# A four-stage transformer kernel whose fourth GEMM is computed by seven half-size products for eight

## The chip, the cores and the metric

The kernel runs on one core of a Trainium2 chip. The metric is the device time of one execution in microseconds, lower is better; each of the runs below is one measurement of it, and the profile is one execution recorded by the hardware profiler.

## The reference

Float32 attention with 32 global tokens and a local window feeds a gated block, and that feeds a second one. Batch 4, 8 heads of 64, 512 local and 32 global tokens: 2176 tokens of 512 features after attention.

```python
attn = concat([softmax(q_g @ k_all.T / 8) @ v_all,
               softmax([q_l @ k_g.T / 8, mask(q_l @ k_l.T / 8)]) @ [v_g, v_l]])
x = attn as rows of 512
h = x @ w_in                       # first GEMM, 512 -> 1024
s = h * softmax(h)
y = layernorm(s) * g_ln @ w_out    # second GEMM, 1024 -> 512
h = y @ w2_in                      # third GEMM, 512 -> 2048
g = h * clip(h + 3, 0, 6) / 6
out = g @ w2_out                   # fourth GEMM, 2048 -> 512
```

## The kernel before

The 2176 tokens are 17 units of 128 (16 local, one global). A unit passes through attention, the first GEMM (L804), the softmax product and the layer norm, and the second GEMM (L864, whose left operand comes by DMA transposes `lT<-l`, issued on SP). The weights lie in DRAM as 64-bit words; `decode` (L404 to L422) makes float32 of a loaded block of 512 columns with one ScalarE and several VectorE or GpSimd instructions, `norm` (L436) sums its squares, `power_scale` (L366 to L375, with the tiny matmul of L372 that adds over partitions) makes a power of two of the sum, and `split` (L444 to L456) makes two float16 values, a high part and a rest, of each number. With such pairs a product is three terms: high x high, high x rest, rest x high.

The third and fourth GEMMs are in `second(gi)` (L950 to L1006). The units are taken in `GROUPS` of 4, 4, 3, 3, 3. For each group, 16 chunks `f` of 128 of the 2048 features are gone through: 12 matmuls of the third GEMM (L968; 4 slices of 128 features x 3 terms, 512 or 384 token columns) fill a PSUM tile `S`; ScalarE makes relu(h + 3) of it (L972), VectorE min(., 6) x h (L974), ScalarE the high half (L977), VectorE the rest (L979); the fourth GEMM (L988) adds 3 terms per unit, of 512 output columns each, into one accumulator bank per unit (tags V, V, Y, Y). After the last chunk the accumulators are scaled (L1003 on VectorE, L1005 on ScalarE) and stored (L1006). Group 0 does its fourth GEMM with fp32r pairs; `convert` (L938 to L948) makes float16 pairs of those weights for groups 1 to 4, in buffers of earlier stages, after `token_scale` has one scale of all tokens. `prep_w2(f)` (L881 to L908) prepares chunk `f` of both weights.

The order on every engine is set by class `Plan`: each step has an engine, a cost, what it reads and writes, the buffers it needs and a rank, and a list scheduler places steps by rank as their inputs, buffers and engines come free. A table `RK` of ranks, `MODE` strings (which engine or variant a block gets) and `SLOTS` (how many buffers) are constants of the file. All loads, transposes and stores are issued on SP's one queue, in the planned order.

## Time and profile before

| | us |
|---|---|
| three runs | 724.06, 727.26, 728.14 |
| median | 727.26 |
| span of the profiled execution | 722.6 |
| TensorE (PE) busy in it | 668.1 |
| VectorE (DVE) busy | 456.6 |
| ScalarE (ACT) busy | 410.3 |
| GpSimd (POOL) busy | 166.7 |

The profiled execution's own time is not given beside its span. Busy time counts matmuls, copies and the like, not waits or the issue of DMAs. A line name such as L968 is a line of the kernel before; `S<-ybig,w2i` reads output, then inputs. A matmul's row gives the time from its start to its modelled end, and since matmuls overlap, the price of one in a stream is the distance to the next. The mean granted clock of TensorE over the span is 0.974 of full speed.

### The profile page before, as it was taken

How to read it: one execution, taken by the hardware profiler on the slowest of the kernel's cores; microseconds unless marked ns; L12 is line 12 of the kernel's file. 1: busy time of each engine (PE TensorE's matmuls, PEld its weight loads, DVE VectorE, ACT ScalarE, POOL GpSimd, SP SyncE). 2: the span in 40 equal slices, each digit the busy share in tenths (PEclk: the TensorE clock that was granted, in tenths of full speed). 3: DMA queues.
4: the chain of work that ended last, by engine and by line, in shares of the span. 5: the costliest groups of instructions: out<-in, count | busy, mean ns of one | idle time of the engine just before them, and what ended most of it. 6: DMA issues, size and time to landing. Idle time of an engine off the chain costs nothing.

```text
span 722.6 us, 11985 instructions
## 1 busy us (share of the span) xinstructions
PE 668.1 (92%) x4488; PEld 412.6 (57%) x4488; DVE 456.6 (63%) x1112; ACT 410.3 (57%) x783; POOL 166.7 (23%) x197
## 2 busy tenths in 40 slices
PE   3665789999999999989999999999999999999997
PEld 2443465676766777566666666444455555555553
DVE  4799878886767788796879987933323233323323
ACT  6767658766566787667667776423333333324323
POOL 7243236531613153633421420000000000000000
PEclk9998759999999999999999999999999999999999
DMA  9998976999799979872835410100010000001001
GB/s 317 251 255 175 213 157 181 212 187 207 202 224 189 173 154 176 140 187 81 197 77 175 146 59 17 43 1 0 1 59 0 1 20 26 0 1 44 1 1 44
DMA packets 155657, 82.93 MB, mean 115 GB/s; under 512 B 132944, under 2 KB 141136, under 8 KB 155600
## 3 DMA queue, kind: packets, MB, share of 16 engines
q1 hardware_dynamic: 155600, 82.18, 48.6%
q8 instruction: 35, 0.57, 0.3%
q14 instruction: 22, 0.18, 0.1%
HBM read 42.55 MB, written 4.46 MB: 65 GB/s over the span
## 4 chain that ended last, share of the span: by engine, by line
PE 75%; DMA 9%; DVE 6%; ACT 4%; issue 2%; POOL 1%; SPq 1%; ACTq 0%; DVEq 0%; POOLq 0%
PE S L968 22%; PE V L988 14%; PE Y L988 10%; PE Y L864 10%; PE H L804 8%; PE S L609 5%; DMA PT<-zone 4%; PE S L644 2%; DMA lT<-l 2%; PE V L736 1%; DMA wd<-in_vm_dram 1%; DVE tm L812 1%; DMA raw<-in_w_in_dram 1%; DMA zone<-in_ki_dram 1%; DVE zone L634 1%
## 5 line engine op out<-in xcount | busy, mean ns | idle before, releaser
L968 PE MATMUL S<-ybig,w2i 128*128 128x384 f16 (+1 forms) x720 | 139.4, 347 | 0.0
L972 ACT ACTIVATE g<-S,three,inv 128x384 f32<-128x384 f32 (+1 forms) x80 | 56.9, 712 | 135.3 <-PE S L968 133.9
L974 DVE SCALAR_TENSOR_TENSOR g<-g,S 128x384 f32<-128x384 f32 (+1 forms) x80 | 48.2, 605 | 126.0 <-ACT g L972 123.8
L968 PEld LDWEIGHTS <-w2i 128*128 128x128 f16 x720 | 69.8, 98 | 63.0 <-issue 2.2
L988 PEld LDWEIGHTS <-gh 128*128 128x128 f16 x624 | 60.6, 98 | 71.7 <-ACT gh L977 3.6
L864 PE MATMUL Y<-lT,wout 128*128 128x256 f16 (+1 forms) x864 | 96.0, 269 | 2.8 <-DMA lT<-l 2.8
L804 PE MATMUL H<-win,xT 128*128 128x512 f16 x384 | 91.8, 386 | 2.2 <-DVE tm L817 1.2
L864 PEld LDWEIGHTS <-wout 128*128 128x128 f16 x864 | 80.3, 99 | 16.2 <-issue 2.8
L979 DVE SCALAR_TENSOR_TENSOR gh<-g,g_scale,gh 128x384 f16<-128x384 f32 (+1 forms) x64 | 41.7, 651 | 41.9 <-ACT gh L977 27.5
L609 PE MATMUL S<-zone 64*128 64x224 f32 x256 | 58.9, 439 | 8.4 <-ACT sg L650 7.0
L977 ACT ACTIVATE gh<-g,g_scale 128x384 f16<-128x384 f32 (+1 forms) x64 | 41.0, 641 | 41.0 <-DVE g L974 41.0
L804 PEld LDWEIGHTS <-xT 128*128 128x128 f16 x384 | 36.2, 99 | 45.5 <-issue 9.0
L619 ACT ACTIVATE e<-e,sa 128x224 f32<-128x224 f32 x128 | 53.1, 471 | 14.3 <-DVE sa L614 14.1
L609 PEld LDWEIGHTS S<-zone 64*128 64x128 f32 x256 | 38.9, 222 | 21.5 <-ACT sg L650 8.5
L614 DVE CUSTOM_DVE_ANT_0 e<-msk,S 128x224 f32<-128x224 f32 x128 | 42.9, 381 | 12.8 <-PE S L609 12.0
L968 PE MATMUL S<-ybig,zone 128*128 128x384 f16 (+1 forms) x240 | 47.2, 347 | 0.0
L988 PE MATMUL V<-raw,gh 128*128 128x512 f16 x144 | 42.8, 379 | 0.0
L634 DVE SCALAR_TENSOR_TENSOR zone<-e,zone 128x896 f16<-128x896 f32 x32 | 36.2, 1130 | 5.4 <-ACT zone L632 2.8
L686 PE MATMUL V<-v,PT 128*128 128x65 f16 x128 | 25.6, 203 | 14.6 <-DMA PT<-zone 14.6
L988 PE MATMUL V<-wd,gh 128*128 128x512 f16 x120 | 35.7, 379 | 0.0
L968 PEld LDWEIGHTS <-zone 128*128 128x128 f16 x240 | 23.3, 98 | 20.9 <-issue 0.6
L644 PE MATMUL S<-zone 128*128 128x128 f32 (+1 forms) x128 | 27.2, 344 | 7.8 <-DVE sa L614 7.6
(226 smaller groups left out, 1297.0 us busy)
## 6 DMA issues: line engine op xcount, KB each, us to landing
raw<-in_w_in_dram SPq DMA_DIRECT2D x24, 512.0 KB, 4.4
raw<-in_w_out_dram SPq DMA_DIRECT2D x24, 512.0 KB, 4.2
zone<-in_ki_dram SPq DMA_DIRECT2D x16, 448.0 KB, 4.2
out_dram<-o SPq DMA_DIRECT2D x17, 256.0 KB, 2.1
zone<-in_qi_dram SPq DMA_DIRECT2D x16, 256.0 KB, 3.0
wd<-in_vm_dram SPq DMA_DIRECT2D x12, 256.0 KB, 4.7
vs<-v SPq DMA_DIRECT2D x24, 64.5 KB, 2.6
vs<-vg SPq DMA_DIRECT2D x16, 64.5 KB, 2.9
```

What stands on the lines that cost most here:

```text
L609: T.matmul(out=S()[:, j], lhsT=p.tile(qk)[d, 2 * hf + j], rhs=p.tile(kk)[d, 2 * hf + j], start=True, stop=True)
L614: V.tensor_tensor_reduce(out=p.tile(ek)[:, KC * (2 * j + jj):KC * (2 * j + jj) + KC], in0=msk[:, mtyp], in1=S()[:, j], scale=-0.125, scala ...
L619: A.activation(out=p.tile(ek)[:, c:c + KC], in_=p.tile(ek)[:, c:c + KC], func=AF.Exp, bias=p.tile(sa)[:, h:h + 1], scale=-1.0)
L634: vop(dve(896), lambda ev=ev, pk=pk: V.scalar_tensor_tensor(out=p.tile(pk)[:, 1, :, 0:KC], in0=ev(), scalar=PSC, in1=p.tile(pk)[:, 0, :, 0 ...
L644: T.matmul(out=p.tile(gk)[:, 0:n], lhsT=p.tile(gq)[:, 2 * hf + j], rhs=p.tile(kk)[:, 2 * hf + j, 0:n], start=(j == 0), stop=(j == 1))
L804: T.matmul(out=p.tile(hk)[:, 512 * n:512 * n + 512], lhsT=(p.tile(xk) if xb else xgT)[:, 4 * a + k], rhs=win16[:, w, k, 512 * n:512 * n + ...
L864: T.matmul(out=Y()[:, m2], lhsT=wout16[:, w, k, 128 * m:128 * m + 128], rhs=p.tile(lk)[:, 8 * a + k, 0:n], start=(z == 0 and k == 0), stop ...
L968: T.matmul(out=p.tile(hk)[:, 0:n], lhsT=p.tile(wk)[:, w, k], rhs=y16[:, a, k, c0:c0 + n], start=(z == 0 and k == 0), stop=(z == 2 and k == 3))
L972: aop(act(n, 2), lambda hk=hk, gk=gk, iv=iv: A.activation(out=p.tile(gk)[:, 0:n], in_=p.tile(hk)[:, 0:n], func=AF.Relu, bias=three, scale= ...
L974: vop(dve(n), lambda hk=hk, gk=gk: V.scalar_tensor_tensor(out=p.tile(gk)[:, 0:n], in0=p.tile(gk)[:, 0:n], scalar=6.0, in1=p.tile(hk)[:, 0: ...
L979: vop(dve(n, 1), lambda rk=rk, gk=gk, gs=gs: V.scalar_tensor_tensor(out=p.tile(rk)[:, 1, 0:n], in0=p.tile(gk)[:, 0:n], scalar=gs, in1=p.ti ...
L988: T.matmul(out=p.tile(accs[t]), lhsT=p.tile(rk)[:, a, 128 * t:128 * t + 128], rhs=p.tile(ok)[:, w], start=(f == 0 and z == 0), stop=(f == ...
```

## The change

The fourth GEMM is done in a Strassen scheme on 2 x 2 blocks. The units are taken in pairs (8 pairs and the single unit 16, `NG` = 9 groups), and the chunks in pairs too (8 pairs, `pi`). For one chunk pair and one pair of units, the product of a 2 x 2 arrangement of blocks (two units by two chunks) with another (two chunks by two halves of 256 output columns) is formed from 7 products of a sum of token blocks with a sum of weight blocks, instead of 8 products of single blocks. Each product is 3 matmuls of 256 columns (the three float16 terms). Seven accumulators of 256 columns fill four banks, called a, b (tags V) and d, c (the two halves of the former tile H of the first GEMM, so they exist only after it).

- The sums on the token side are made by VectorE (L1051: 128, 256 and 256 columns), so that high part (L1060) and rest (L1062) have 896 columns in place of 512. The sums on the weight side, five of 256 columns per chunk pair, are made in the preparation (VectorE or GpSimd by a mode string), and a pair's weights are split into nine blocks.
- The work is in two phases of four chunk pairs (`PHASES`). Phase 0 goes through all groups with chunk pairs 0 to 3 and stores scaled partial sums to DRAM (`part`, L1160); phase 1 goes through them again with chunk pairs 4 to 7, loads the partial sums (`pp`, L1110) and adds them. The weights of pairs 4 to 7 are prepared during phase 0, which frees the memory that nine blocks a pair need.
- At the end of a phase of a pair of units, ten instructions combine the seven sums (ScalarE L1137 and L1138 for a and d, VectorE L1139 to L1157, in phase 1 two adds on GpSimd, L1146 and L1149).
- A mode string says which of the 18 group-phases are quick: 15 are; one pair of phase 0 and the single unit (both phases) keep single blocks of 512 columns (L1091).
- There is no fp32r and no conversion any more. The token scale is taken twice, of units 0 to 3 and of units 4 to 16. The scale of each chunk's output weights needs its own tiny matmul (16 more).
- The third GEMM's matmuls have 256 token columns (a pair of units), 24 per chunk pair and group (L1031).
- Planned costs of GpSimd and of a DMA's latency are raised, and all ranks and modes are new, so the order before the second blocks changes too.

```diff
-GROUPS = [(0, 4), (4, 4), (8, 3), (11, 3), (14, 3)]
+PHASES = [(0, 4), (4, 4)]
+TOKENS = [(0, 4), (4, 17)]
+NP = NF // 2
+NG = NU // 2 + 1
...
+    for z in range(2):
+        p.tag(f"H{z}", [p.slots["H"]["tiles"][0][:, 512 * z:512 * z + 512]], "hb")
...
+        for c, (x, y, op) in enumerate([((0, 1), (1, 0), ALU.add), ((0, 1), (0, 0), ALU.add), ((1, 1), (1, 0), ALU.add), ((0, 0), (1, 0), ALU.subtract), ((1, 1), (0, 1), ALU.subtract)]):
+            on, cost, E = (vop, dve(256), V) if MODE["wc"][pi] == "v" else (gop, pool2(256), G)
+            on(cost, lambda E=E, c=c, x=x, y=y, op=op: E.tensor_tensor(out=p.tile(ck)[:, c], in0=half(*x), in1=half(*y), op=op), r=dk, w=[ck], b=[ck] + dk, rank=rank)
...
+    PRODUCTS = {2: ("a", 0, 2, 1), 5: ("a", 1, 3, 7), 1: ("d", 0, 1, 2), 4: ("b", 0, 6, 6), 3: ("b", 1, 0, 5), 6: ("c", 0, 4, 3), 7: ("c", 1, 5, 4)}
+    BANKS = dict(a="V", b="V", c="H0", d="H1")
...
+        units = [2 * q, 2 * q + 1] if 2 * q + 1 < NU else [2 * q]
+        nu = len(units)
...
+            for f in range(2):
+                for z, ch in enumerate(passes(4)):
+                    def mm(f=f, z=z, ch=ch, h=h, wk_=wi[f]):
+                        for k, a, w in ch:
+                            T.matmul(out=h()[:, f], lhsT=p.tile(wk_)[:, w, k], rhs=y16[:, a, k, c0:c0 + n], start=(z == 0 and k == 0), stop=(z == 2 and k == 3))
...
+                for o, x, y, op in (((2, 1, 1), (1, 1, 1), (7, 1, 1), ALU.add), ((3, 2, 1), (0, 2, 1), (7, 2, 1), ALU.add), ((5, 2, 1), (0, 2, 8), (1, 2, 6), ALU.subtract)):
...
+                src = lambda gk=gk: p.tile(gk)[:, 128:1024]
+                m = 896
...
+                def mm4(ms, zs, rk=rk, wk=wk, at=at, last=last):
+                    for m_ in ms:
+                        bk, half, ai, bi = PRODUCTS[m_]
+                        for z in zs:
+                            a, w = TERMS[z]
+                            T.matmul(out=p.tile(bank[bk])[:, 256 * half:256 * half + 256], lhsT=p.tile(rk)[:, a, 128 * ai:128 * ai + 128], rhs=p.tile(wk)[:, w, bi],
+                                     start=(at == 0 and z == 0 and half == 0), stop=(last and z == 2), skip_group_check=True)
...
+                    for ms, bk in (((2, 5), "a"), ((1,), "d"), ((4, 3), "b"), ((6, 7), "c")):
+                        pe(3 * len(ms) * mm16(256), lambda mm4=mm4, ms=ms: mm4(ms, range(3)), r=[rk, wk] + before, w=[("oo", key, bk)], b=[rk, wk] + accs, rank=rank + 0.5)
...
+            if ph:
+                gop(pool2(512), lambda: G.tensor_tensor(out=ob(1, 2), in0=ev(0, 2), in1=pb(1, 2), op=ALU.add), r=sx + [pk], w=[("sp", key)], b=[ek, ok, pk], rank=rank)
...
+        for z, u in enumerate(units):
+            to = out if ph else part
+            dma(262144, lambda z=z, u=u, to=to: SP.dma_start(out=to[u], in_=p.tile(ok)[:, z]), r=[("of", key, z)], w=[("st", ph, q, z)], b=[ok], rank=rank)
...
+        if u == SLOTS["AT"]:
+            prep_w2i(0, RK["w2"], "V")
+            prep_w2o(0, RK["w2"] + 0.1, "V")
...
+    for pi in range(1, 4):
+        prep_w2i(pi, RK["w2z"] + 2 * pi, "V")
+        prep_w2o(pi, RK["w2z"] + 2 * pi + 0.1, "V")
+    for pi in range(4, NP):
+        prep_w2i(pi, RK["w2b"] + 4 * pi, "Y")
+        prep_w2o(pi, RK["w2b"] + 4 * pi + 0.1, "Y")
...
+    for ph in range(2):
+        for q in range(NG):
+            second(ph, q)
```

TensorE in the fourth GEMM (`gh` are the split token sums, `ws` the weights of a chunk pair; a row is one matmul or its weight load). Before, in a middle group of three units:

```order
L988 LDWEIGHTS gh0_3598
L988 MATMUL V0_71<-zone_102,gh0_3598 128x512
L988 LDWEIGHTS gh0_3598
L988 MATMUL V1_72<-zone_102,gh0_3598 128x512
L988 LDWEIGHTS gh0_3598
L988 MATMUL Y1_75<-zone_102,gh0_3598 128x512
```

and after, the first six of the seven products of one term in a middle chunk pair of phase 1, where V1 is bank a, V0 bank b, and H0 the tile of d and c:

```order
L1074 MATMUL V1_72<-ws6_0_4606,gh_0_3740 128x256
L1074 LDWEIGHTS gh_0_3740
L1074 MATMUL V1_72<-ws6_0_4606,gh_0_3740 128x256
L1074 LDWEIGHTS gh_0_3740
L1074 MATMUL H0_73<-ws6_0_4606,gh_0_3740 128x256
L1074 LDWEIGHTS gh_0_3740
L1074 MATMUL V0_71<-ws6_0_4606,gh_0_3740 128x256
L1074 LDWEIGHTS gh_0_3740
L1074 MATMUL V0_71<-ws6_0_4606,gh_0_3740 128x256
L1074 LDWEIGHTS gh_0_3740
L1074 MATMUL H0_73<-ws6_0_4606,gh_0_3740 128x256
```

Three banks of whole units have become products of half the columns; at the last chunk pair of a phase they come product by product: a, d, b, c, with d and c on the same tile.

VectorE at the end of a group. Before, one eviction stands between the chunks of the next group:

```order
L974 SCALAR_TENSOR_TENSOR g2_3595<-g2_3595,S1_70 128x384
L979 SCALAR_TENSOR_TENSOR gh1_3599<-g2_3595,g_scale_150,gh1_3599 128x384
L1003 TENSOR_SCALAR o4_3604<-V1_72,inv6_147 128x512
L974 SCALAR_TENSOR_TENSOR g0_3593<-g0_3593,S0_69 128x384
L979 SCALAR_TENSOR_TENSOR gh0_3598<-g0_3593,g_scale_150,gh0_3598 128x384
```

and after, at the end of a quick group of phase 1 (`ev` holds evicted sums, `inv6` the scale):

```order
L1041 SCALAR_TENSOR_TENSOR g_0_3738<-g_0_3738,S0_69 128x2x256
L1051 TENSOR_TENSOR g_0_3738<-g_0_3738 128x128
L1051 TENSOR_TENSOR g_0_3738<-g_0_3738 128x256 x2
L1139 SCALAR_TENSOR_TENSOR ev_0_3745<-V0_71,inv6_1_1_236,ev_0_3745 128x256
L1141 SCALAR_TENSOR_TENSOR ev_0_3745<-V0_71,inv6_1_1_236,ev_0_3745 128x256
L1155 SCALAR_TENSOR_TENSOR ev_0_3745<-H0_73,inv6_1_1_236,ev_0_3745 128x256 x2
L1147 SCALAR_TENSOR_TENSOR o_1_3744<-V0_71,inv6_1_1_236,o_1_3744 128x512
L1062 SCALAR_TENSOR_TENSOR gh_2_3742<-g_0_3738,acol1_1_235,gh_2_3742 128x896
L1157 TENSOR_TENSOR o_1_3744<-ev_0_3745 128x256 x2
```

The evictions of c (from H0) and b (from V0) stand between the next chunk pair's sums and its rest.

SP's queue behind the last transpose of the second GEMM's operand. Before, the last 15 weight loads follow one another:

```order
L845 DMA_TRANSPOSE lT_97<-l_95 128x16x128
L398 DMA raw_83<-in_w_out_dram 128x1024
L398 DMA raw_84<-in_w_in_dram 128x4x256
L398 DMA raw_85<-in_w_out_dram 128x1024
L398 DMA raw_83<-in_w_in_dram 128x4x256
L398 DMA raw_84<-in_w_out_dram 128x1024
```

and after, they are spread between stores and loads of partial sums:

```order
L849 DMA_TRANSPOSE lT_99<-l_97 128x16x128
L410 DMA raw_83<-in_w_in_dram 128x4x256
L410 DMA raw_84<-in_w_out_dram 128x1024
L410 DMA raw_85<-in_w_out_dram 128x1024
L1160 DMA part<-o_3743 128x512 x2
L1110 DMA pp_4594<-part 128x512
L410 DMA raw_83<-in_w_in_dram 128x4x256
L1110 DMA pp_4594<-part 128x512
L410 DMA raw_84<-in_w_in_dram 128x4x256
L1160 DMA part<-o_3744 128x512 x2
L1110 DMA pp_4595<-part 128x512 x2
```

A weight load now stands behind a store that waits for its group's results.

## Rows read from the trace of the kernel before

**Rows 1.** The page: span, and each engine's busy time, share and instructions.
```profile
span 722.6 us, 11985 instructions
...
PE 668.1 (92%) x4488; PEld 412.6 (57%) x4488; DVE 456.6 (63%) x1112; ACT 410.3 (57%) x783; POOL 166.7 (23%) x197
```

**Rows 2.** Stretches: length; busy us (count) of PE, PEld, DVE, ACT, POOL; clock; DMA share; GB/s.
```profile
0.00:100.00 100.00, 59.06 (x365) 40.54 (x365) 78.28 (x221) 68.11 (x153) 42.07 (x49) 0.89 0.88 228
100.00:370.00 270.00, 260.55 (x2374) 184.69 (x2375) 208.65 (x567) 188.59 (x378) 107.26 (x136) 0.97 0.86 180
370.00:440.00 70.00, 69.93 (x326) 46.23 (x324) 60.72 (x139) 49.56 (x95) 17.36 (x12) 1.00 0.30 98
440.00:460.00 20.00, 20.00 (x93) 10.79 (x91) 19.92 (x45) 17.02 (x27) 0.00 (x0) 1.00 0.15 54
460.00:718.00 258.00, 257.90 (x1337) 130.25 (x1336) 88.27 (x143) 86.28 (x130) 0.00 (x0) 1.00 0.03 11
```

**Rows 3.** Waits of TensorE: total us, times, longest us.
```profile
PE V L686 <- DMA PT<-zone: 14.6, 7, 5.6
PE Y L372 <- DVE am_v L537: 9.0, 1, 9.0
PE S L644 <- DVE sa L614: 7.6, 4, 3.2
```

**Rows 4.** The chain that ended last: start us, us, what.
```profile
448.22 1.40 PE Y L988 x6
...
505.42 5.18 PE S L968 x24
...
570.90 3.90 PE S L968 x24
```

**Rows 5.** TensorE's timeline, 347 to 373 us: start, us, instruction, idle before.
```profile
348.37 10.65 PE L864 MATMUL Y<-lT,wout 128*128 128x256 f16 x96 [0.71 <-DMA lT<-l]
358.86 0.28 PE L372 MATMUL H<-inv,ones 128*128 128x1 f32 x2
...
364.78 5.52 PE L864 MATMUL Y<-lT,wout 128*128 128x128 f16 x96 [1.38 <-DMA lT<-l]
370.14 2.75 PE L968 MATMUL S<-ybig,zone 128*128 128x512 f16 x12
```

**Rows 6.** The last microseconds, all engines.
```profile
717.15 1.46 PE L988 MATMUL V<-junk,gh 128*128 128x512 f16 x6
...
718.65 0.69 ACT L1005 ACTIVATE o<-V,inv 128x512 f32<-128x512 f32 x1 [0.61 <-PE V L988]
```

**Rows 7.** Groups by shape: count, busy us, mean ns, idle before.
```profile
L634 DVE SCALAR_TENSOR_TENSOR zone<-e,zone 128x896 f16<-128x896 f32 x32 | 36.2, 1130 | 5.4 <-ACT zone L632 2.8 <-POOL zone L629 2.3
...
L974 DVE SCALAR_TENSOR_TENSOR g<-g,S 128x512 f32<-128x512 f32 x32 | 21.7, 682 | 37.0 <-ACT g L972 37.0
...
L632 ACT ACTIVATE zone<-e 128x896 f16<-128x896 f32 x19 | 17.9, 943 | 4.7 <-DMA PT<-zone 4.5
...
L871 ACT ACTIVATE ybig<-Y 128x256 f16<-128x256 f32 x2 | 0.8, 383 | 2.5 <-PE Y L864 2.5
```

**Rows 8.** VectorE's timeline, while it decodes weights in group 0.
```profile
402.64 0.42 DVE L411 TENSOR_SCALAR wd<-wd 128x512 int32<-128x512 int32 x1
402.97 0.42 DVE L410 TENSOR_SCALAR wd<-wd 128x512 f32<-128x512 f32 x1
403.31 0.68 DVE L417 SCALAR_TENSOR_TENSOR wd<-raw,wd 128x512 int32<-128x512 int32 x1
403.91 0.42 DVE L411 TENSOR_SCALAR wd<-wd 128x512 int32<-128x512 int32 x1
```

**Rows 9.** All engines, 430.5 to 433 us: VectorE and GpSimd side by side.
```profile
430.57 0.73 DVE L979 SCALAR_TENSOR_TENSOR gr<-g,inv,gr 128x512 fp32r<-128x512 f32 x1
...
431.19 1.29 POOL L354 TENSOR_TENSOR w2o<-wd,w2o 128x512 fp32r<-128x512 f32 x1 [2.94 <-ACT w2o L901]
431.23 1.80 DVE L445 SCALAR_TENSOR_TENSOR w2i<-wd,psc,w2i 128x512 f16<-128x512 f32 x1
```

More of the change, by code (lines that the diff above doesn't have):

```diff
@@ L316, in attention_solu_swish_kernel @@
     zone_at[0] = 0
[L317 removed]
+    carve("ws1", 1, [128, 2, 9, 256], F16, "z")
+    for f in range(2, 8):
         carve(f"w2i{f}", 1, [128, 2, 4, 128], F16, "z")
[L319 removed]
     tags(right1, "e", SLOTS["e"], [128, 4 * KC], F32, "a")
@@ L368, in power_scale, with total @@
             lambda: V.tensor_scalar(out=si[:, 2:3], in0=p.tile(pk).bitcast(I32)[:, 0:1], scalar1=24, scalar2=23, op0=ALU.logical_shift_right, op1=ALU.logical_shift_left),
[L369 to L372 removed]
+            lambda: V.tensor_scalar(out=si[:, 0:1], in0=si[:, 2:3], scalar1=-1.0, scalar2=float((205 - down) << 23), op0=ALU.mult, op1=ALU.add),
+            lambda: V.tensor_scalar(out=si[:, 1:2], in0=si[:, 2:3], scalar1=1.0, scalar2=float((49 + down) << 23), op0=ALU.mult, op1=ALU.add),
+        ]
+        n = len(cols)
+        def total():
+            for c in range(n):
+                T.matmul(out=p.tile(pk)[:, 0:1], lhsT=ones, rhs=cols[c], start=c == 0, stop=c == n - 1)
+        pe(0.12 * n, total, r=rk, w=[("t1", z)], b=[pk], rank=rank)
         vop(0.13, steps[0], port=False, r=[("t1", z)], w=[("t2", z)], b=[pk], rank=rank)
@@ L915, in token_scale @@
+    g_scale = [const.tile([128, 3], F32, name=f"g_scale{z}") for z in range(len(TOKENS))]
+    def token_scale(z, rank, bank):
+        u0, u1 = TOKENS[z]
+        n = u1 - u0
+        t = const.tile([128, n + 1], F32, name=f"tsc{z}")
+        si = g_scale[z].bitcast(I32)
+        pk = p.buf(("tsc", z), bank)
+        x = t[:, 0:n]
+        lf, ls = lfac[:, u0:u1], lsq[:, u0:u1]
         steps = [
-            lambda: V.scalar_tensor_tensor(out=x, in0=lfac, scalar=2.0 ** -30, in1=lfac, op0=ALU.mult, op1=ALU.mult),
@@ L921, in token_scale @@
         ]
-        prev = [("y3", u) for u in range(NU)]
-        for z, fn in enumerate(steps):
-            vop(dve(NU), fn, r=prev, w=[("tsc", z)], rank=rank)
-            prev = [("tsc", z)]
-        pe(0.12, lambda: T.matmul(out=p.tile(pk)[:, 0:1], lhsT=ones, rhs=t[:, NU:NU + 1], start=True, stop=True), r=prev, w=["tsc5"], b=[pk], rank=rank)
-        vop(0.13, lambda: V.tensor_scalar(out=si[:, 2:3], in0=p.tile(pk).bitcast(I32)[:, 0:1], scalar1=26, scalar2=23, op0=ALU.logical_shift_right, op1=ALU.logical_shift_left), port=False, r=["tsc5"], w=["tsc6"], b=[pk], rank=rank)
@@ new lines, in token_scale @@
+        prev = [("y3", u) for u in range(u0, u1)]
+        for k, fn in enumerate(steps):
+            vop(dve(n), fn, r=prev, w=[("tsc", z, k)], rank=rank)
+            prev = [("tsc", z, k)]
+        pe(0.12, lambda: T.matmul(out=p.tile(pk)[:, 0:1], lhsT=ones, rhs=t[:, n:n + 1], start=True, stop=True), r=prev, w=[("tsc5", z)], b=[pk], rank=rank)
+        vop(0.13, lambda: V.tensor_scalar(out=si[:, 2:3], in0=p.tile(pk).bitcast(I32)[:, 0:1], scalar1=26, scalar2=23, op0=ALU.logical_shift_right, op1=ALU.logical_shift_left), port=False, r=[("tsc5", z)], w=[("tsc6", z)], b=[pk], rank=rank)
@@ L1084, in open_region @@
             pool = late_pools.enter_context(tc.tile_pool(name="left2", bufs=1, side="left", reuse_waits="tile"))
-            for f in range(SLOTS["NR"], NF):
-                p.slots[f"w2o{f}"]["tiles"] = [pool.tile([128, 2, DM], F32R, name=f"w2o{f}")]
+            shapes = {"pp": ([128, 2, DM], F32)}
+            for f in range(8, NF):
+                shapes[f"w2i{f}"] = ([128, 2, 4, 128], F16)
+        for pi in range(2, NP):
+            if p.slots[f"ws{pi}"]["region"] == g:
+                shapes[f"ws{pi}"] = ([128, 2, 9, 256], F16)
+        for name, (shape, dt) in shapes.items():
+            p.slots[name]["tiles"] = [pool.tile(shape, dt, name=f"{name}_{i}") for i in range(p.slots[name]["n"])]
     for i in p.seq:
```

385 lines of the change are left out of this document (228 added, 157 removed).

## The prediction

> **What bounds the kernel now.** I read the page's head, then the busy time by stretch, the waits of TensorE, its timeline, and last the other engines row by row. TensorE (PE) is busy for 668.1 of 722.6 us [rows 1], and by stretch [rows 2] all of its idle time is early: 40.9 us in the first 100 us and 9.5 us in the next 270. From 370 us on it runs without a gap (347.8 of 348 us) at a granted clock of 1.00, that is, at the 2.4 GHz level. What idle time there is comes from the attention stage: a DMA transpose (14.6 us), the decoding of a weight (9.0), VectorE's row scaling (7.6) and others [rows 3]. So the kernel has two parts: a start with several owners, and from 370 us a stretch in which only the number and the price of TensorE's matmuls count. The change is in the second, but it rewrites the order of the first.
>
> The prices of one matmul are in the chain and the timeline. Six fp32r matmuls of 512 columns take 1.40 us, so .2335 each; 24 float16 ones of 512 columns take 5.18 (.216) and 24 of 384 columns 3.90 (.1625) [rows 4]. At 256 columns 96 matmuls, each with its own weight load, run from 348.37 to 358.86, so .1093 each; at 128 columns 96 run from 364.78 to 370.14, so .0558 [rows 5]. Price goes with columns, all the way down: halving a matmul's columns costs 1% more per column. That is what a scheme of more and smaller products needs.
>
> **The change part by part.** *Third GEMM.* Before: 16 chunks x 12 matmuls x 2 groups at .216 and x 3 groups at .1625, 82.9 + 93.6 = 176.5 us. After: 8 groups of two units, 16 x 12 x 8 = 1536 matmuls at .1093 = 167.9, and one single unit, 192 at .0558 = 10.7: 178.6. **+2.1.**
>
> *Fourth GEMM.* Before: group 0 with 192 fp32r matmuls, 44.8 us, the other 13 units 16 x 3 x 13 = 624 at .216, 134.8: 179.6 us. After: 15 of the 16 pair-phases take 4 chunk pairs x 7 products x 3 terms = 84 matmuls of 256 columns, 15 x 84 x .1093 = 137.7; one plain pair 48 x .216 = 10.4; two plain singles 24 x .216 each, 10.4: 158.5. **-21.1.** All of it is on the path [rows 2]. Seven products for eight alone would give an eighth of 179.6, or 22.5.
>
> A rule speaks against small matmuls: the Trainium skill, "TensorE: Matmul & The Clock Gate", section "Back-to-back issue gap", gives a sustained stream of weight loads and matmuls about 81 ns apart at 128 columns. By it the 192 matmuls of the single unit would cost 4.8 us more (an estimate from that page). The trace has 55.8 ns on the same kind of stream [rows 5], so the measurement decides and nothing is added.
>
> *Column sums.* 16 more of the tiny fp32 matmuls that sum a weight's squares; two of them lie .28 apart in TensorE's stream [rows 5], so .14 each: **+2.2.**
>
> *Accumulators.* A quick group uses four banks, a, d, b, c in this order at its last chunk pair, and c and d lie in the two halves of one former tile. In the order the first c product waits until d has been evicted, and d's eviction stands on ScalarE behind a's. An eviction starts .2 us after the last matmul's slot (718.65 against 717.15 + 6 x .216) and takes .69 for 512 columns [rows 6]; 256 columns take .38 [rows 7]. So c can start .20 + .69 + .38 = 1.27 us after a's last matmul, while d and b fill 9 x .1093 = .98. A stall of .29 at 15 groups: **+4**; 0 if ScalarE gets there sooner, 9 if it is held up by a third of a 896-column copy (943 ns, [rows 7]) each time. The next group's first products find 20 or more third-GEMM matmuls (2.2 us) ahead of them, which covers the VectorE evictions.
>
> *VectorE.* In the new phase 0 the weights of chunk pairs 1 to 7 are still being decoded while quick groups run. A quick chunk pair costs VectorE .68 (512 columns, PSUM), about .9 for the sums of blocks (640 columns at the .68 per 512 of [rows 8]) and 1.13 for the 896-column rest [rows 7]: 10.8 a group, and 3.1 for six evictions (256 columns like the .38, 512 like the .68). The 13.9 us are some 13 in slots, since rows follow .08 closer than they last [rows 8], against 4 x 45 x .1093 = 19.7 us of TensorE. Over groups 1 to 8 of phase 0 TensorE has 149.5 us of work (7 pairs x 96 x .1093, 55.1 for six quick groups, 10.4 for the plain pair, 10.6 for the single) and VectorE 78 + 9 for the groups and 38 for three pairs' preparation at 12.7 (four blocks decoded at .33 + .34 + .60 and a bit more, 6.3, [rows 8]; 3328 columns of rests at .68 per 512, 4.4; 2.0 for block sums): 125. The cover is thin but has been so before: in 440 to 460 us VectorE was busy for 19.92 of 20 us and TensorE for 20.00 [rows 2]. **+3**, 0 to 10.
>
> *GpSimd.* It gets 21 decoding adds of 512 at 1.29 [rows 9], 15 block sums of 256 at about .75 and 6 scalings at about .95 (both scaled from that row): some 44 us of phase 0. It has idle time for that; what it does to VectorE is the first rival.
>
> *Partial sums.* 17 stores and 17 loads of 256 KB more on a queue that fills 3% of the DMA engines from 460 us on [rows 2], and the loads are issued two groups ahead of use: **0**. On SP's queue the stores now stand between the last weight loads (the order shows it); a store waits for its group's end, and a weight load behind it is needed a group or more later, so 0 again; a load that comes late by a store's wait costs at most one group, as in the second rival.
>
> *Last group.* A single unit ends the program instead of three. Per chunk pair its TensorE work is 48 x .0558 + 6 x .216 = 4.0 us for two passes through ScalarE and VectorE, so it stays covered; the last result is one instead of three: **+1**, 0 to 2, for the load of partial sums joined to its eviction.
>
> *The start.* All ranks are new, so the 50 us of idle time before 370 us fall elsewhere. The two waits for the last transposes (.71 + 1.38, [rows 5]) have other work ready beside them now, since group 0 needs the token scale of its own four units only: **-2**. No row prices the rest; the longest single wait for a transpose is 5.6 us [rows 3], so I bound it by one such wait either way, -6 to +6.
>
> Sum: 2.1 - 21.1 + 2.2 + 4 + 3 + 0 + 1 - 2 = **-10.8**. The profiled span of 722.6 becomes 711.8. The page gives no time for that execution beside its span; the three runs (724.06, 727.26, 728.14) lie 1.5 to 5.5 above it, the median 4.7. I carry the 4.7 over: **716.5 us**.
>
> **The rivals.** *GpSimd stops VectorE (slower).* An add of 512 columns on GpSimd takes 1.29 us, and the VectorE instruction of 512 columns beside it 1.80, where one just before took .73: 1.07 us lost for 1.29 of GpSimd [rows 9]. If each of the 44 us cost VectorE one, it would have 169 us of work against 149.5 of TensorE: 20 us in place of my 3, and 716.5 + 17 = **734**. It decides once more than 149.5 - 125 = 24.5 of the 44 us fall on VectorE. For it: such a collision in this very stretch. Against it: 107 us of GpSimd and 209 of VectorE share 100 to 370 us with TensorE at 96% [rows 2]. The Trainium skill, "SBUF — State Buffer", section "Who interferes with whom", has this as a lock on ports that the two engines share, which a VectorE instruction with one SBUF input escapes. By that rule the slowed row is the expected one, and the instructions that read PSUM, half of a group's work here, are not touched; so the rival has a chance, but not the likelier one.
>
> *The start or the group changes eat it (no change).* 17 group changes with single-buffered accumulators at 1 us each in place of my 4 in all would add 13: 729. A start that loses 10 where I gain 2 gives 728. For it: the evictions of a change now wait for each other across two engines. Against it: before, the four accumulators were single as well, and TensorE never stopped [rows 2]. About **727 to 730**.
>
> *All is covered (faster by more).* ScalarE reaches d in time and VectorE hides: 716.5 - 4 - 3 = 709.5, and a start that gains 6: **705**.
>
> *The change doesn't do what it says:* the order shows 84 products of 256 columns in 15 pair-phases, so I give it nothing.
>
> **How the numbers follow.** .5 on the forecast, .15 on the larger gain, .17 on no change and .18 on the slower one. The forecast's own range is 710 to 723: sum of the part bounds that go together (stall 0 to 9, VectorE 0 to 10). The range that holds 8 of 10 takes in most of the larger gain and of no change: **706 to 731**. A measurement of this kernel tells about 0.5% (3.6 us) from no change, so faster means under 723.6 and slower over 730.9: **.65, .17, .18**.
>
> **What would show it.** Right: the new fourth-GEMM lines sum to about 158 us of TensorE and the third to 179; no TensorE idle time in the second phase beyond .3 us a group, put down to ScalarE's eviction of d; partial loads landing long before use. Wrong: TensorE idle in phase 0, with waits on VectorE's copies or on the weights (the first rival); more idle time before the last transpose than 50 us (the second); 256-column matmuls over .12 us apart, which would undo the saving itself.

## The result, and the profile after

The changed kernel took 734.57 us in the median of four runs (729.4 to 736.63), the kernel before, beside it, 725.86 (724.06 to 728.14): a ratio of 1.0107, 95% interval 1.0068 to 1.0146. Run again for this study, six more runs gave 733.58 (729.31 to 738.7), a ratio of 1.0104 [1.0069, 1.0140]. It is slower by 1%; the forecast was 716.5, faster by 1.5%, and 734.6 lies above its range of 706 to 731. The profiled execution is the quickest of the first four, 729.4 us; its span against the 722.6 of [rows 1]:

```profile
span 727.6 us, 15092 instructions
...
PE 653.5 (90%) x5828; PEld 516.9 (71%) x5828; DVE 588.3 (81%) x1396; ACT 429.9 (59%) x780; POOL 219.2 (30%) x239
```

TensorE has 14.6 us less to do, as wanted, and is idle for longer. VectorE has 131.7 us more. To see where, I cut both executions at the last matmul of the second GEMM (the end of "the start") and at the last matmul of all. Stretches of the changed kernel (columns as in [rows 2]):

```profile
0.00:380.97 380.97, 318.72 (x2802) 230.55 (x2803) 311.48 (x844) 263.22 (x540) 147.82 (x181) 0.94 0.85 187
380.97:723.80 342.83, 334.78 (x3029) 286.37 (x3026) 276.04 (x552) 166.68 (x240) 71.33 (x58) 1.00 0.18 59
```

and of the kernel before:

```profile
0.00:370.30 370.30, 319.92 (x2741) 225.47 (x2742) 286.94 (x787) 256.69 (x530) 149.33 (x185) 0.95 0.86 193
370.30:718.61 348.31, 348.14 (x1749) 187.12 (x1746) 169.52 (x325) 152.90 (x252) 17.36 (x12) 1.00 0.09 31
```

The phases are 5.5 us shorter than the groups they replace, and the start is 10.7 us longer, in this execution all of it TensorE's idle time (62.3 us against 50.4; the busy time is 1.2 us less). The same two numbers for every run of the study but run 4, from one profiled execution each (idle is length less busy time; each ratio is to runs of the kernel before made beside it, whose medians lie between 725.9 and 727.0):

| run | start, us | idle in it | clock in it | phases, us | median | ratio to before, 95% |
|---|---|---|---|---|---|---|
| before | 370.3 | 50.4 | .95 | 348.3 | 725.9 | |
| changed | 381.0 | 62.3 | .94 | 342.8 | 734.6 | 1.0107 [1.0068, 1.0146] |
| changed, again (13) | 384.5 | 58.8 | .93 | 342.8 | 733.6 | 1.0104 [1.0069, 1.0140] |
| 1 plain | 384.3 | 61.2 | .89 | 348.6 | 736.5 | 1.0116 [1.0072, 1.0160] |
| 2 start of before | 393.1 | 66.1 | .91 | 346.6 | 744.8 | 1.0244 [1.0191, 1.0296] |
| 3 modes in before | 387.4 | 63.6 | .93 | 382.9 | 776.9 | 1.0684 [1.0642, 1.0727] |
| 5 plain, no sums | 384.2 | 59.3 | .93 | 348.6 | 735.6 | 1.0114 [1.0076, 1.0153] |
| 6 norm engines | 385.5 | 64.4 | .90 | 342.7 | 734.7 | 1.0113 [1.0086, 1.0140] |
| 7 d's own bank | 390.4 | 61.8 | .90 | 338.3 | 726.5 | 1.0016 [0.9985, 1.0047] |
| 8 sums in before | 387.4 | 60.0 | .93 | 373.1 | 766.4 | 1.0543 [1.0513, 1.0574] |
| 9 start of before, late weights | 386.3 | 62.9 | .90 | 365.7 | 756.9 | 1.0428 [1.0406, 1.0450] |
| 10 start of after in before | 393.4 | 68.0 | .91 | 348.0 | 747.6 | 1.0297 [1.0280, 1.0314] |
| 11 late weights | 388.7 | 65.7 | .89 | 362.1 | 756.2 | 1.0429 [1.0391, 1.0467] |
| 12 d's own bank, all sums | 386.8 | 61.7 | .90 | 338.2 | 730.5 | 1.0055 [1.0039, 1.0071] |
| 14 three pairs first | 381.1 | 61.6 | .91 | 365.6 | 754.6 | 1.0394 [1.0358, 1.0430] |
| 15 weights two units later | 399.7 | 69.9 | .91 | 340.4 | 744.7 | 1.0228 [1.0190, 1.0267] |
| 16 weights by lower rank | 396.9 | 73.4 | .90 | 340.4 | 748.8 | 1.0275 [1.0227, 1.0322] |

**Who TensorE waits for in the start** (columns as in [rows 3]):

```profile
PE S L648 <- DVE sa L618: 28.7, 15, 7.5
PE S L613 <- DVE sa L618: 14.9, 5, 4.0
PE Y L382 <- DVE am_v L541: 8.9, 1, 8.9
...
PE V L690 <- DMA PT<-zone: 0.7, 1, 0.7
```

L618 is VectorE's row maximum over the attention scores, which frees the scores' bank. TensorE waits 43.6 us for it, 32.7 of them before 120 us. In the kernel before the same wait was 7.6 us [rows 3] and this row:

```profile
PE S L609 <- DVE sa L614: 1.0, 2, 0.7
```

The wait for transposes, 14.6 us in [rows 3], is down to .7: the new order cured what had been the largest wait and made another.

One place can be read off. VectorE's timeline behind 212 us (start, us, instruction, idle before):

```profile
213.65 0.75 DVE L422 TENSOR_SCALAR wd<-wd 128x512 f32<-128x512 f32 x2
214.31 0.76 DVE L423 TENSOR_SCALAR wd<-wd 128x512 int32<-128x512 int32 x2
214.99 1.29 DVE L429 SCALAR_TENSOR_TENSOR wd<-raw,wd 128x512 int32<-128x512 int32 x2
216.19 0.68 DVE L431 SCALAR_TENSOR_TENSOR wd<-raw,wd 128x512 int32<-128x512 int32 x1
216.79 0.42 DVE L433 TENSOR_SCALAR raw<-raw 128x512 int32<-128x512 int32 x1
217.13 0.68 DVE L360 TENSOR_TENSOR x<-xn,x 128x512 f16<-128x512 f32 x1
217.73 0.38 DVE L618 CUSTOM_DVE_ANT_0 e<-msk,S 128x224 f32<-128x224 f32 x1
```

and TensorE's:

```profile
212.30 1.03 PE L613 MATMUL S<-zone 64*128 64x224 f32 x8
218.48 1.23 PE L648 MATMUL S<-zone 128*128 128x128 f32 x4 [5.14 <-DVE sa L618]
```

`wd` is a block of the last two GEMMs' weights: for 3.5 us VectorE decodes the first chunk pair while the row maxima, whose scores have been ready since 213.3, and TensorE behind them stand. The stretch 180 to 220 us has 7.2 us of such idle time, and its granted clock is .93, so part of it runs at the lower of the clock's two levels (1.2 GHz; 1.00 in the column is 2.4 GHz throughout):

```profile
180.00:220.00 40.00, 32.76 (x295) 24.04 (x293) 34.01 (x91) 25.76 (x56) 15.00 (x17) 0.93 0.83 161
```

The same stretch of the kernel before:

```profile
180.00:220.00 40.00, 38.63 (x382) 28.50 (x381) 28.07 (x82) 24.83 (x53) 14.87 (x23) 1.00 0.89 215
```

**The phases.** One end of a group in phase 1, all engines, the rows that matter:

```profile
613.65 0.69 ACT L1137 ACTIVATE ev<-V,inv 128x512 f32<-128x512 f32 x1 [1.19 <-PE V L1074]
613.72 0.82 PE L1074 MATMUL V<-ws,gh 128*128 128x256 f16 x6
614.24 0.47 ACT L1138 ACTIVATE ev<-H,inv 128x256 f32<-128x256 f32 x1
...
614.75 0.82 PE L1074 MATMUL H<-ws,gh 128*128 128x256 f16 x6 [0.22 <-ACT ev L1138]
...
615.04 0.48 DVE L1141 SCALAR_TENSOR_TENSOR ev<-V,inv,ev 128x256 f32<-128x256 f32 x1
615.30 2.17 PEld L1031 LDWEIGHTS <-w2i 128*128 128x128 f16 x20
615.40 2.35 PE L1031 MATMUL S<-ybig,w2i 128*128 128x256 f16 x20
```

This is the forecast stall: a's eviction, then d's, and c waits. b's six matmuls end their slots at 613.72 + 6 x .1093 = 614.38 and c starts at 614.75, .37 us lost (the row's .22 counts from the modelled end). Counted so, 14 of the 15 quick groups lose .31 to .75 us each, 5.4 in all; the fifteenth loses nothing.

### The profile page after: what moved, and what is told of

Read it like the earlier page. It is cut to its first block, busy times and chain, and to the rows that moved or that the text cites. A ratio compares the mean times of both kernels' runs of the same rounds, so it can differ in the third digit from the quotient of the medians.

```text
span 727.6 us, 15092 instructions
## 1 busy us (share of the span) xinstructions
PE 653.5 (90%) x5828; PEld 516.9 (71%) x5828; DVE 588.3 (81%) x1396; ACT 429.9 (59%) x780; POOL 219.2 (30%) x239
## 4 chain that ended last, share of the span: by engine, by line
PE 58%; DVE 23%; ACT 9%; DMA 4%; issue 4%; POOL 1%; SPq 1%; ACTq 0%; POOLq 0%; DVEq 0%
PE S L1031 16%; PE Y L868 10%; PE H L808 8%; PE V L1074 7%; PE H L1074 6%; PE S L613 4%; DVE g L1051 3%; DVE gh L1062 3%; PE S L648 2%; DVE zone L638 2%; ACT gh L1060 2%; DVE g L1041 2%; DMA zone<-in_ki_dram 2%; PE V L1091 1%; DVE e L618 1%
## 5 line engine op out<-in xcount | busy, mean ns | idle before, releaser
L1074 PEld LDWEIGHTS <-gh 128*128 128x128 f16 x1260 | 121.9, 98 | 27.2 <-issue 5.7
L1060 ACT ACTIVATE gh<-g,acol 128x896 f16<-128x896 f32 (+2 forms) x72 | 69.3, 963 | 100.8 <-DVE g L1051 95.2
L1031 PE MATMUL S<-ybig,w2i 128*128 128x256 f16 (+1 forms) x1080 | 124.2, 267 | 0.1
L1031 PEld LDWEIGHTS <-w2i 128*128 128x128 f16 x1080 | 101.2, 98 | 12.3 <-issue 0.2
L1074 PE MATMUL V<-ws,gh 128*128 128x256 f16 x636 | 106.4, 273 | 3.6 <-ACT gh L1060 2.2
L1062 DVE SCALAR_TENSOR_TENSOR gh<-g,acol,gh 128x896 f16<-128x896 f32 (+2 forms) x72 | 78.3, 1089 | 35.7 <-ACT gh L1060 35.6
L1074 PE MATMUL H<-ws,gh 128*128 128x256 f16 x477 | 94.2, 272 | 3.3 <-ACT ev L1138 3.3
L1039 ACT ACTIVATE g<-S,three,inv 128x512 f32<-128x512 f32 (+1 forms) x72 | 53.9, 749 | 54.9 <-PE S L1031 46.4
L1031 PE MATMUL S<-ybig,zone 128*128 128x256 f16 (+1 forms) x648 | 76.4, 268 | 3.2 <-ACT zone L448 1.6
L1051 DVE TENSOR_TENSOR g<-g 128x128 f32<-128x128 f32 x180 | 69.4, 438 | 1.2
L1031 PEld LDWEIGHTS <-zone 128*128 128x128 f16 x648 | 60.5, 99 | 11.5 <-ACT zone L448 2.9
L1041 DVE SCALAR_TENSOR_TENSOR g<-g,S 128x512 f32<-128x512 f32 (+1 forms) x72 | 47.0, 653 | 19.4 <-ACT g L1039 19.0
L613 PEld LDWEIGHTS S<-zone 64*128 64x128 f32 x256 | 35.2, 238 | 26.3 <-DVE sa L618 16.8
L1146 POOL TENSOR_TENSOR o<-ev,pp 128x512 f32<-128x512 f32 x8 | 10.2, 1275 | 140.7 <-ACT ev L1137 140.7
L618 DVE CUSTOM_DVE_ANT_0 e<-msk,S 128x224 f32<-128x224 f32 x128 | 43.1, 380 | 7.9 <-PE S L613 7.3
```

The source lines that it names most:

```text
L613: T.matmul(out=S()[:, j], lhsT=p.tile(qk)[d, 2 * hf + j], rhs=p.tile(kk)[d, 2 * hf + j], start=True, stop=True)
L618: V.tensor_tensor_reduce(out=p.tile(ek)[:, KC * (2 * j + jj):KC * (2 * j + jj) + KC], in0=msk[:, mtyp], in1=S()[:, j], scale=-0.125, scala ...
L1031: T.matmul(out=h()[:, f], lhsT=p.tile(wk_)[:, w, k], rhs=y16[:, a, k, c0:c0 + n], start=(z == 0 and k == 0), stop=(z == 2 and k == 3))
L1039: aop(act(2 * n, 2), lambda gview=gview, h=h, iv=iv: A.activation(out=gview(), in_=h(), func=AF.Relu, bias=three, scale=iv), r=prev + [("i ...
L1041: vop(dve(2 * n), lambda gview=gview, h=h: V.scalar_tensor_tensor(out=gview(), in0=gview(), scalar=6.0, in1=h(), op0=ALU.min, op1=ALU.mult ...
L1051: on(cost(128 * o[1]), lambda E=E, gk=gk, o=o, x=x, y=y, op=op: E.tensor_tensor(out=blocks(gk, *o), in0=blocks(gk, *x), in1=blocks(gk, *y) ...
```

## The experiments

**1. No Strassen, all else kept.** One string, `st`, is set to `'n'` throughout: the same two phases, the same weight preparation, plain products.

```diff
-st='ssnsssssnssssssssn'
+st='nnnnnnnnnnnnnnnnnn'
```

> All 18 group-phases by plain products of 512 columns, in two phases as in the changed kernel. Theory (the start lost the time, the products gain what was forecast): 15 x (96 x .216 = 20.7 minus 84 x .1093 - 9.2 x 0 ...) that is 15 x (48 x .216 - 84 x .1093 = 10.4 - 9.2) = 17.8 us more TensorE work, less the 3.3 us of waits on the eviction of d and part of the 4.6 us of waits on the token sums: 10 to 17 us slower than the changed kernel, about 747 us, with the start as in it (62 us of TensorE idle before the last matmul of the second GEMM). Rival (the scheme's own extra VectorE work and evictions eat its gain): within 5 us of the changed kernel's 734.6.

736.5 us and not 747: the time stays near the changed kernel's, and by medians the scheme seems worth 2 us. By stretch it is worth 5.7: the phases take 348.6 us against 342.8, in starts whose order on VectorE agrees up to 330 us. Of 17.8 us of TensorE work saved, 5.4 go to the wait for d and 4.6 to waits on the split token sums (L1060, L1062; 3.8 of it in phase 0); some 2 are not accounted for. What the scheme gains does not make up for the start, which is as long without its products.

**2. The start's ranks (24), modes (`bits`, `win`, `wout`, `v`, `x`, `xl`, `l`, `P`) and planned costs of the kernel before, in the changed one;** three of the edits:

```diff
-l='dddgdaddagdddgada'
+l='gdagaagdaagagaagd'
...
-g1c=-205.31, g1t=-91.45, g2=0.98, g2e=-267.83
+g1c=-49.47, g1t=-58.32, g2=4.74, g2e=-61.23
...
-lag=2.1 if trans else 2.0
+lag=0.8
```

> The changed kernel with the engine choices, ranks and planned costs of the start taken from the kernel before. Theory (the new order of the start costs 12 us): TensorE idle before the last matmul of the second GEMM falls from 62 to about 50 us and the time by about 11, to 723. Rival (the loss is in the two phases, in waits and the clock): idle in the start changes by under 4 us and the time stays above 730.

744.8: worse, not better; the start took 393.1. Transposes are waited for again (20.6 us), and the first weights, which the changed kernel prepares from the tenth unit on, still stand between. Neither theory had said that.

**3. The same eight mode strings of the changed kernel, alone, in the kernel before.**

```diff
-l='gdagaagdaagagaagd'
+l='dddgdaddagdddgada'
```

> The kernel before with only the new choices of engine for the start (which engine decodes, splits and normalizes; ten layer-norm steps of 1024 columns on VectorE that were on GpSimd or ScalarE). Theory A (VectorE is overloaded in the attention stage by these choices): the kernel before loses 8 to 12 us, about 736. Theory B (ranks and planned costs set the loss): within 4 us of 725.9.

776.9, five times the loss that even theory A expected, 34.6 us of it after the second GEMM, where TensorE waits 22.3 us on a weight's norm (L436). Engine choices and ranks are fitted to each other in such a plan: exchanging one of them alone measures the misfit, not the part. This made me keep the order itself in the next runs and change only what is issued.

**4. d in a bank of its own, planned.**

```diff
-BANKS = dict(a="V", b="V", c="H0", d="H1")
+BANKS = dict(a="V", b="V", c="H0", d="Y")
```

> The changed kernel with the sum d in a bank of its own (one of the two that the second GEMM used), so that c no longer shares a tile with it. Theory: the 3.3 us of TensorE waits on ScalarE's eviction of d go, 2 to 4 us faster, about 731. Rival (the wait moves to the next one in the row of evictions): no change within 1 us.

796.2 us (1.0926 [1.0873, 1.0979]). The tiny sums of the later weights use the same tag, the planner hands a tag's buffers out in program order, and in the profiled execution (804.8 us) TensorE waited 60.3 us on norms (L440) before the tiny matmuls. So this run says nothing on the wait for d.

**5. The order of run 1, without the weight sums.** The instructions of the five sums and the split of their 1280 columns are not issued (plain products do not read them).

```diff
-E.tensor_tensor(out=p.tile(ck)[:, c], in0=half(*x), in1=half(*y), op=op)
+None
```

> The plain two-phase kernel of the first experiment with its order kept, instruction by instruction, but without the work that only the scheme needs in the weight preparation: the sums of weight blocks and the split of their 1280 columns. In the changed kernel that was some 12 us of VectorE before the last matmul of the second GEMM (6.0 for the sums, five of 1280 columns 7.7 in all, half of them early). Theory (this work delays the row maxima for which TensorE waits in the attention stage): the start gets 4 to 10 us shorter than in the first experiment (384.3) and the time falls to about 729. Rival (the order of the rest sets the start): start and time within 2 us of the first experiment's 736.5.

735.6 and a start of 384.2 against 384.3 (idle 59.3 against 61.2), though VectorE was busy for 300.5 us in it and not 310.8. The scheme's own extra work on the weights is not what lengthens the start: its first sum begins at 219.1 us, behind the wait that ends at 218, and without it the start is as long.

**6. The layer norm's centring step on its engines of before, same order.** The step stays where it was planned; only the engine that gets it changes.

```diff
-E.tensor_scalar(out=p.tile(uk), in0=p.tile(uk), scalar1=-float(DFF), scalar2=c(3), op0=ALU.mult, op1=ALU.add)
+(G if real == "g" else V).tensor_scalar(out=p.tile(uk), in0=p.tile(uk), scalar1=-float(DFF), scalar2=c(3), op0=ALU.mult, op1=ALU.add)
```

> The changed kernel with its order kept, but the 1024-column centring step of the layer norm on the engine that it had in the kernel before: 7 net steps, 6 us, leave VectorE for ScalarE and GpSimd. Theory (VectorE's load in the attention stage costs the start): 2 to 6 us faster, about 731. Rival (what counts is where an instruction stands in the order, or GpSimd is slow to do it): no change or slower.

734.7 against 734.6: no change, the rival's side. VectorE was busy for 307.9 us in the start, against 311.5 and 313.1 in the changed kernel's two profiles, so some 4 to 5 us less of its work at these places give nothing.

**7 and 12. d in its own bank, same order.** The planned order stays; only the tile that d's matmul and eviction name is another, and the later tiny sums share the bank beside it. In run 7 the first group overwrote sums of the second GEMM that were still to be read, so some of its output values are wrong; run 12 leaves that group as it was.

```diff
-T.matmul(out=p.tile(bank[bk])[:, 256 * half:256 * half + 256], ...
+T.matmul(out=(p.slots["Y"]["tiles"][1] if bk == "d" and key != (0, 0) else p.tile(bank[bk]))[:, 256 * half:256 * half + 256], ...
```

> The changed kernel with its order kept, the sum d in a bank of its own (the tiny matmuls of the later weights all use the other of the two banks). Theory: the 3.3 us of waits on ScalarE's eviction of d go, TensorE's stretch after the second GEMM gets 3 us shorter than 342.8. Rival (the next eviction in the row, by VectorE, ends hardly earlier): under 1 us.

> The seventh experiment again, with the first group of phase 0 left as in the changed kernel (there the second GEMM's last sums were still being read from the bank). Theory: TensorE's stretch after the second GEMM is 4 to 5 us shorter than the changed kernel's 342.8, and the time 4 to 5 us under that of the changed kernel run beside it. Rival (the seventh experiment's 726.5 came from its runs' starts): under 2 us.

The phases of run 12:

```profile
386.77:724.96 338.19, 332.95 (x3028) 286.31 (x3026) 275.58 (x552) 166.43 (x240) 71.12 (x58) 1.00 0.18 60
```

4.6 us shorter than 342.83, 4.5 in run 7: the wait on d is real and worth nearly what its slots say (5.1 without the first group), more than the 3.3 us that the waits view counts. The time is 730.5 against the changed kernel's 733.6 on the same chip, 3.1 less by medians where 4 to 5 were expected, and within the spread of the latter's runs. Run 7's one profile has the same phases, so its 726.5 probably differs by its starts: its runs lie between 725.4 and 734.3, and the profiled one, 734.3, has the longest start of all with that order. Run 12 is the best version with all values right, and still .55% [.39, .71] slower than the kernel before.

**8. The sums' VectorE work added to the kernel before:** six additions of 200 columns per chunk, results unused, planned at nearly nothing.

```diff
+for z in range(6):
+    V.tensor_tensor(out=scr, in0=p.tile(d2)[:, 0:200], in1=p.tile(d2)[:, 256:456], op=ALU.add)
```

> The kernel before plus six VectorE additions of 200 columns per chunk where its output weights are prepared (about 1.9 us a chunk, 30 us in all, the amount that the scheme's sums and wider rests add; the planner is not told of them; their results are not used). Theory (extra VectorE work in the preparation is on the path in the start): 4 to 10 us slower, the most of it before the last matmul of the second GEMM. Rival (hidden beside TensorE): under 2 us.

766.4: 39.5 us slower; in the profiled execution 17 in the start and 25 in the groups. The 96 additions were not the 30 us intended: they take .44 to .47 us each, 44.5 in all, so they cost nearly all of their own time. The kernel before, in its order, had hardly any room on VectorE where weights were prepared. With run 5 this reads: work on VectorE costs nothing or nearly all of itself, by its place.

**9, 11, 15, 16. The first weights later.** Run 9 is run 2 with the first pair behind the last attention unit; 11 the changed kernel with the same move; 15 run 12 with the pair two units later; 16 run 12 with its rank behind the row maxima (`w2=150`). The edit of run 11, of which run 15 has `AT=12` and run 9 also `GATE=6`:

```diff
-pp=2, GATE=2, AT=10)
+pp=2, GATE=2, AT=18)
```

> The changed kernel with the start of the kernel before (engine choices, ranks, planned costs), and now the first pair of weights also prepared as late as there, after the last attention unit. The orders agree until the first eviction of the second GEMM. Theory (the new order of the attention stage alone costs the start some 12 us): idle up to 220 us falls from 54.5 to 43 to 46 and the last matmul of the second GEMM ends near 373 in place of 381 to 386; if the phases then find their weights in time, about 722. Rival (the two phases need four chunk pairs of weights within some 20 us, so VectorE's work on them has to lie before, and the start gains what the first group then loses): the waits on weights in the first groups rise by 8 us or more and the time stays above 730.

> The changed kernel with its own start, but the first pair of weights prepared after the last attention unit and not from 190 us on. The two waits of 2.1 and 5.1 us at 185 and 218 us, in which VectorE decodes weights before the row maxima for which TensorE waits, are then without that work. Theory: they go (7 us less idle up to 220 us), and the weights come later: the first groups wait for them by more than that. Rival: the waits stay, since the order of the rest makes them.

> The kernel of the twelfth experiment (d in its own bank) with the first pair of weights prepared two attention units later. Theory (the decoding of that pair ahead of the row maxima makes the two waits at 185 and 218 us and the lower clock around them, but it must be ready when the phases begin): the waits go and the stretch 180 to 240 us runs at 1.00, the start ends 3 to 8 us earlier than the twelfth experiment's 386.8, and the weights come in time for most of it: 723 to 730. Rival (as in the eleventh experiment, what is moved later is missed later): 735 or more.

> The same kernel with the first pair's place unchanged but its rank below that of the row maxima (150 in place of -63.8), so that a ready row maximum goes first. Theory: as in the run before, the waits at 185 and 218 us go; 723 to 730. Rival: the order before it shifts as well (it parts from the changed kernel's at an earlier row), the start stays at 381 to 390, 730 or more.

All four are slower: 756.9, 756.2, 744.7, 748.8. Run 11 shows why. The stretch of the two waits, and the one in which the phases begin:

```profile
180.00:220.00 40.00, 37.37 (x345) 25.64 (x343) 26.39 (x73) 24.91 (x51) 13.72 (x20) 1.00 0.88 174
...
360.00:420.00 60.00, 42.15 (x374) 34.99 (x372) 56.18 (x126) 35.84 (x61) 17.93 (x16) 0.83 0.40 112
```

and the latter in the changed kernel:

```profile
360.00:420.00 60.00, 57.32 (x554) 49.68 (x552) 52.19 (x112) 33.05 (x55) 16.42 (x11) 0.99 0.30 89
```

The idle time at 180 to 220 us falls from 7.2 to 2.6 and the clock there is 1.00, as the theory had it; then TensorE stands for 17.9 of 60 us where the phases begin, against 2.7, while VectorE is busy for 56.2 of them (from 340 to 440 us its largest waits are put down to ScalarE's split of the token sums, 5.3, a weight's norm, 4.9, and a transpose, 4.2). Run 9 loses 16.8 us in that stretch in the same way. Run 15 avoids it and pays between 240 and 340 us (13.9 us idle against 2.8), run 16 at 240 to 260. Run 2, with the pair early in the order of before, has 4.8 us of idle time at 180 to 220 us, and run 9, with it late, 1.6. The work is wanted before the phases begin, and at each of the places tried the start or the phases lost more than the two waits had cost.

**10. The new start in the kernel before:** run 2 the other way round.

```diff
-g1c=-49.47, g1t=-58.32, g2=4.74, g2e=-61.23
+g1c=-205.31, g1t=-91.45, g2=0.98, g2e=-267.83
...
-lag=0.8
+lag=2.1 if trans else 2.0
```

> The kernel before with the start of the changed one: engine choices, ranks and planned costs. The orders agree with the changed kernel's until its first pair of weights. Theory (that order is the cost): TensorE idle up to 180 us 47 us, as in the changed kernel, against 41.9 before. Rival (the order is no worse, the work of the weights between it is): 42 to 43. Its later part is planned for another kernel, so the total says little; in the third experiment it lost 50 us.

45.9 us idle at 180 us, between the two: 41.9 in the kernel before. But run 9, with the order of before up to there, has 46.1, and the changed kernel's own order 47.3 and 44.8 in its two profiles. So up to 180 us the orders can't be told apart by one execution each. From 180 to 220 us run 10 is idle for 5.5 us, 4.7 of it on row maxima, though VectorE decodes no weight of the last two GEMMs there (before: 1.4 us idle; run 11: 2.6): the new order can wait on row maxima in that stretch without the first weights too.

**13. The changed kernel again,** with no edit.

> The changed kernel itself, beside the others: 730 to 736 us. What the runs differ by should go with the mean granted clock, as the start of one and the same order took 381 to 390 us in the profiles so far.

729.3 to 738.7 over six runs, wider than expected; the profiled one has a start of 384.5 us. The mean granted clock does not order them: the two slowest (736.0 and 738.7) have the lowest, .945 and .947, but the quickest, 729.31, has .957 and a run of 733.86 has .965.

**14. Three chunk pairs in phase 0, five in phase 1.**

```diff
-PHASES = [(0, 4), (4, 4)]
+PHASES = [(0, 3), (3, 5)]
```

> The changed kernel with three chunk pairs in phase 0 and five in phase 1, so that only three pairs of weights are wanted when the phases begin. Theory (weights that must be ready early push VectorE's work before the row maxima and before the end of the second GEMM): 12 us of VectorE leave the start, which gets 2 to 6 us shorter than the 381 to 386 of the changed kernel; phase 0 is then a quarter shorter (some 40 us) while VectorE has one pair more to prepare in it, so TensorE waits there more than the 4.6 us of the changed kernel. Rival (the start is set by its order in the attention stage, not by the weights): the start within 2 us.

754.6. The start is 381.1, no shorter than 381.0. But VectorE's busy time in it did not fall by the 12 us of the theory either (312.5 us against 311.5): the planner put other work there. So the run shows that asking for fewer pairs does not shorten the start under this planner, and not what a start with less VectorE work would take. The phases lose 22.8 us, where TensorE waits on norms (14.3 us in five waits) and on weights, as the theory said of phase 0.

## Why the prediction was wrong

**The step that failed is "The start: -2", bounded at 6 either way.** It measured +10.7 us in the profiled execution and +14.2 in the second. With the measured start in its place the sum would have been +1.9, so this step decides the sign.

An estimate for the medians comes near the second: nearly every run on record takes 1.7 to 2.0 us more than its span, so with the lengths of phases and end as profiled the median runs (725.86 and 734.57) have starts of about 372 and 386 us. It also means that the profiled execution before took about 724.5 us, one of the quick ones, so most of the 4.7 us carried from span to time was the spread of its runs.

I read the kernel before as "a start with several owners" and priced the rewritten order by the waits that I could see go; I bounded it by the longest wait for a transpose (5.6), though its idle time had room for more and VectorE's load was in [rows 2]. The 7.6 us that I took for VectorE's row scaling in [rows 3] is this same wait for row maxima, and the 9.0 that I took for the decoding of a weight is the norm of attention's values (L537).

What took its place: TensorE waits for VectorE's row maxima for 43.6 us in place of 8.6, and VectorE, 287 us busy in the old start, has 311 in the new one. That load alone does not set the start: with 294 and 297 us (runs 9 and 11) TensorE's idle time was 62.9 and 65.7. About half of the lost 11.9 us of idle time, 5.9, lies at 180 to 220 us, and most of it goes with the first weights (timeline above; runs 11, 15 and 16 take it away there and lose more elsewhere; but run 10 waits there without them). Another 5.2 lies before 120 us in this execution and 1.6 in the second; what makes it is not settled, since the orders can't be told apart there (runs 9 and 10). That it is neither the sums' work (run 5) nor the norm's engines (6) is shown; run 14 does not settle the number of pairs. Six other plans (2, 9, 11, 14 to 16) did not bring the start back to 370 us with these phases, so what would is open.

**The phases were right in kind and 3.1 us off.** From the second GEMM's last matmul to the end of the span, the terms add to -8.8; measured 352.3 to 346.6, -5.7. The items below leave about 1 us of the difference open. (The sum that gives "710 to 723" is wrong too: with a stall of 9 and 10 us for VectorE the upper end is 728.5.)

- Third and fourth GEMM, -19.0: right. A group of phase 1 repeats every 20.03 us against 45 x 4 x .1093 = 19.67 and the stall; 256 columns stayed at .1093.
- The stall on d, +4 (.29 each): mechanism right, mostly .31 to .37 each, 5.4 in all. d's eviction takes .467 (L1138) where I took .383 from [rows 7]: the .08 too little. The row taken has a constant scale, d's eviction one from memory.
- VectorE in phase 0, +3: 4.6 us of waits on the split token sums, 3.8 of them in phase 0.
- The last group, +1: the span ends 3.8 us after the last matmul, 4.0 before; 0.
- The partial sums, 0: right. No wait on `pp` or `part` appears.

**The rivals.** The time came out where the first rival had it (734), and not by its mechanism. GpSimd was busy for 51 us of phase 0, near the 44 assumed, and VectorE's instructions with two SBUF inputs are slower there. Groups of VectorE in phase 0, 381 to 560 us:

```profile
L1062 DVE SCALAR_TENSOR_TENSOR gh<-g,acol,gh 128x896 f16<-128x896 f32 x28 | 33.7, 1203 | 9.1 <-ACT gh L1060 9.1
L1051 DVE TENSOR_TENSOR g<-g 128x256 f32<-128x256 f32 x58 | 28.7, 534 | 0.0
L1041 DVE SCALAR_TENSOR_TENSOR g<-g,S 128x512 f32<-128x512 f32 x32 | 21.8, 681 | 3.4 <-ACT g L1039 3.1
```

and in phase 1, 575 to 715 us, where GpSimd has two adds a group:

```profile
L1062 DVE SCALAR_TENSOR_TENSOR gh<-g,acol,gh 128x896 f16<-128x896 f32 x28 | 32.2, 1150 | 23.3 <-ACT gh L1060 23.3
L1051 DVE TENSOR_TENSOR g<-g 128x256 f32<-128x256 f32 x54 | 20.3, 418 | 0.0
L1041 DVE SCALAR_TENSOR_TENSOR g<-g,S 128x512 f32<-128x512 f32 x27 | 18.5, 683 | 13.3 <-ACT g L1039 13.3
```

534 against 418 ns, 1203 against 1150, and no change for L1041, which reads PSUM (681, 683). That agrees with the Trainium skill, "SBUF — State Buffer", section "Who interferes with whom", by which a VectorE instruction with two SBUF inputs contends with GpSimd's reads and one with a single SBUF input does not. No run changed GpSimd's share alone, so the cause is not shown apart from the phase. With the 128-column sums (419 against 292 ns) it makes some 12 us of VectorE, half of the 24.5 from which it would decide. The second rival named the right place, "a start that loses 10 where I gain 2", gave 728 for it and came nearest; I gave it too small a chance, and the group changes that I put beside it cost 5.4 us, near the forecast's 4 and not its 17.

## What to carry to other kernels

When a change rewrites a planned order, price the stage before it by how full the engines that feed TensorE are there, not by the waits of the old order alone: here VectorE was busy for 77% of the start, and moving its work on the first weights moved waits rather than removing them. Saved matmuls count only in the stage where TensorE sets the pace; compare stages cut at the same instruction, since medians (736.5 and 734.6) hid a gain of 5.7 us. To test one part of a planned kernel keep the order and change what is issued: exchanging a table of the plan alone cost up to 50 us by itself.
